# Two attention and MLP layers on one core: V of the first two token tiles from raw x, mended afterwards with column sums and norm rows

## The chip, the cores and the metric

The kernel runs on one core of one Trainium2 chip. The metric is the device time in microseconds (us) of one launch. Of the kernel before there are three runs with a median of 1616.25 us (1616.17 to 1616.3). A core has engines with instruction streams of their own: TensorE (PE) multiplies matrices into PSUM, VectorE (DVE), ScalarE (ACT) and GpSimd (POOL) work on vectors, SyncE (SP) issues most DMAs; ACT issues some too.

## The reference

x is 2048 tokens of D = 1024 in bf16. All is done twice, with the same weights:

```python
x = x + _A_ref(_layernorm(x), wqkv, wo)
x = x + _B_ref(_layernorm(x), W_gate, W_up, W_down)

# _A_ref: 32 heads of 32; each token looks at 8 keys: itself and 2, 4, ... 14 back
qkv = x @ wqkv                         # q, k, v
logits = einsum("bhsd,bhswd->bhsw", q, k[idx]) * Dh ** -0.5   # masked where idx < 0
o = einsum("bhsw,bhswd->bhsd", softmax(logits), v[idx])
return o @ wo
# _B_ref: F = 3584
h = relu(x @ W_gate) * (x @ W_up)
return h @ W_down

# _layernorm: (x - mean) / sqrt(var + 1e-5), no scale, no offset
```

## The kernel before

**Tiling.** The tokens lie in 4 blocks of 512, each of 4 tiles of 128 tokens; D lies in KC = 8 chunks of 128. x stays in SBUF, a token per partition. For a product the normalized block is turned, so that D lies on the partitions: xnT, 4 tiles x 8 chunks of 128x128. Blocks 1 to 3 are turned by DMA transposes on SP. Q, K and V come as [128 of D, 512 tokens] with a weight slab (1 MB, 512 columns or, for Q, K and block 0's V, half of the rows) as the stationary operand. The logits are 8 products of Q with a shifted K on DVE, added up over the head's dimensions: first in DVE (`prod_sum_steps`, tiles t, ac, s), then on PE by `head_mm`, eight products with a selection matrix into a two-bank PSUM tile L. `softmax_steps` does the softmax from L on DVE and ACT; `pv_steps` multiplies with V and sums on DVE; the result goes to DRAM (o_d) and comes back turned (oT) for the products with wo, whose results DVE adds to x.

**What sets the order.** All steps stand in a list `ev` with due times in us, in units of GRP = 1.73 (eight products of 512 columns); the list is sorted and emitted. Helpers keep each engine in that order: `dv` (L101) for DVE, `sp_dma` (L115) for SP, `pe_group` and `mm` (L124, L131) for PE, so that all products have line L132 in the profile, and most DVE operations L106. Weight slabs go through a ring of five buffers: a sixth is loaded when the first is free. PSUM has six one-bank tiles named "acc" (`psum`, taken in turn) and one two-bank tile "L" (`psum_l`), which scratch, turned tiles, bc and the logits share.

**The opening of block 0.** `load_x` brings tile 0's halves on SP and ACT, tile 1 on ACT. `load_slab` brings V's weights in eight pieces of 256 KB on SP, with tiles 2 and 3 of x between them, then Q's first half. `ln_first` (L318) holds the norm of block 0, `v_first` (L482) its V; the event `head` at 0.25 emits both:

- `open_up`: nine products of ones (`scratch`), which nothing reads; tile 0 is centred (mean only) in halves, turned by eight PE transposes (tp) and copied by ACT; tile 1 the same, with its turn between V products (tp_pair, tp_second).
- `chunk(kc, t)`: the eight 128-column V products of chunk kc, tile t. `halves`: both tiles at once, 256 columns.
- 1/sqrt(var) of tiles 0 and 1, split in three bf16 parts (`thirds`), is spread to all partitions by six products with the identity (`spread_rstd`, tile bc, copy rb). `scaled` multiplies V of tiles 0 and 1 with rb as it leaves PSUM; `widen` does the same to xnT for Q and K.
- tiles 2 and 3 are normalized in full (`apply`), turned on PE (tp_pair, 8 transposes each), and copied; tile 3's turn stands in the middle of tile 2's products, sixteen products ahead of where its data is used.

Behind it on PE: Q and K of block 0 (from t_qk0, 128 products), Q and K of block 1, V of blocks 1 and 2, with `head_mm(0)` in the middle of V of block 2 (due at t_v2 + 5.2 GRP), V of block 3, Q and K of block 2 in part, and wo of block 0.

Of the kernel before, what the change touches and what calls it, by code (L numbers as in the profile page):

```python
# [7 lines left out]
BF16 = mybir.dt.bfloat16  # L8
# [9 lines left out]
W = 8  # L18
# [18 lines left out]
def kernel(  # L37
# [123 lines left out]
    k_d = dram.tile([KC, P, S], BF16, name="k_d")  # L161
    s_d = [dram.tile([P, TPB, W, P], BF16, name=f"s_d{i}") for i in range(2)]
# [59 lines left out]
    def load_slab(key, src):  # L222
        shp = list(src.shape)
        t = wring.tile([P, 8 * SLAB], BF16, tag="slab", name="w_" + "_".join(str(k) for k in key))
        tv = t[:, 0:shp[1] * shp[2]].rearrange("p (a b) -> p a b", b=shp[2])
        if key[0] == "v0":
            for i, (k0, k1) in enumerate(((0, 1), (1, 2), (2, 3), (3, 4)) if key[1] == 0 else ((0, 1), (1, 2), (2, 3), (3, 4))):
                if (key[1], i) == (1, 2):
                    load_x(0, [2, 3])
                sp_dma(tv[:, k0:k1, :], src[:, k0:k1, :])  # L230
        else:
            sp_dma(tv, src)
        slab[key] = tv
# [84 lines left out]
    def ln_first():  # L318
        hold = {"xnT": xnT_pool.tile([P, TPB, KC, P], BF16, tag="xnT", name="xnT_first")}
        xna = big_tile([P, TPB, D], "xn_first", True)  # L320
        last = {}
# [20 lines left out]
        def aggr(t):  # L342
            mv = stat_pool.tile([P, 2], F32, tag="mv", name="mv", bufs=4)
            on("v", nc.vector.bn_aggr, mv[:], bst[t][:].rearrange("p a b -> p (a b)"))
            mean[t] = mv[:, 0:1]
            power(t, mv[:, 1:2], 1.0)

        pair = stat_pool.tile([P, 2], F32, tag="rpair", name="rpair", bufs=1)

        def power(t, var, sign):  # L350
            vpe = small("vpe1")
            rstd[t] = pair[:, t:t + 1] if t < 2 else small("rstd1")[:]
            on("g", nc.gpsimd.tensor_scalar, vpe[:], var, sign, EPS, op0=ALU.mult, op1=ALU.add)
            on("g", nc.gpsimd.tensor_tensor, rstd[t], vpe[:], neg_half[:, 0:1], op=ALU.pow)

        def centre():
            parts = [small("part0"), small("part1")]
            on("v", nc.vector.tensor_scalar, xna[:, 0, 0:SLAB], x_tiles[0][:, 0:SLAB], 1.0 / D, None, op0=ALU.mult,
               op1=ALU.add, accum_out=parts[0][:])
            on("a", nc.scalar.activation, xna[:, 0, SLAB:D], x_tiles[0][:, SLAB:D], ACT.Identity, scale=1.0 / D,  # L360
               accum_out=parts[1][:])
            for h in range(2):
                cols = slice(h * SLAB, (h + 1) * SLAB)
                on("v", nc.vector.tensor_scalar, xna[:, 0, cols], x_tiles[0][:, cols], parts[0][:], parts[1][:],
                   op0=ALU.subtract, op1=ALU.subtract)

        def centre_second():
            for h in range(2):
                cols = slice(h * SLAB, (h + 1) * SLAB)
                on("v", nc.vector.tensor_scalar, xna[:, 1, cols], x_tiles[1][:, cols], mean[1], None, op0=ALU.subtract)  # L370

        def square_of(src):
            sq = small("sq1")
            on("a", nc.scalar.activation, xna[:, 3, :], src, ACT.Square, scale=float(D) ** -0.5, accum_out=sq[:])
            return sq

        def act_mean(t):
            mn = small("mean1")
            on("a", nc.scalar.activation, xna[:, t, :], x_tiles[t][:], ACT.Identity, scale=1.0 / D, accum_out=mn[:])
            mean[t] = mn[:]  # L380

        def act_power(t, sq):
            nvar = small("nvar1")
            on("v", nc.vector.scalar_tensor_tensor, nvar[:], mean[t], mean[t], sq[:], op0=ALU.mult, op1=ALU.subtract)
            power(t, nvar[:], -1.0)

        def thirds():
            parts, rest = [], pair
            for i in range(3):
                part = pool["early"].tile([P, 2], BF16, tag=f"part{i}", name=f"part{i}", bufs=1)  # L390
                on("g", nc.gpsimd.tensor_copy, part[:], rest[:])
                parts.append(part)
                if i < 2:
                    left = stat_pool.tile([P, 2], F32, tag="left", name="left", bufs=2)
                    on("g", nc.gpsimd.tensor_tensor, left[:], rest[:], part[:], op=ALU.subtract)
                    rest = left
            return parts

        def spread_rstd():
            hold["rb"] = pool["early"].tile([P, 2, P], F32, tag="rb", name="rb", bufs=1)  # L400
            bc = psum_l.tile([P, W, P], F32, tag="L", name="bc")
            with pe_group():
                for t in range(2):
                    for i, part in enumerate(hold["thirds"]):
                        mm(bc[:, t, :], lhsT=_ap(part, t, [[0, P]]), rhs=ident[:], start=(i == 0), stop=(i == 2))
            on("v", nc.vector.tensor_copy, hold["rb"][:], bc[:, 0:2, :])

        def widen():
            for t in range(2):
                on("v", nc.vector.tensor_tensor, hold["xnT"][:, t, :, :], hold["xnT"][:, t, :, :],  # L410
                   _ap(hold["rb"], t * P, [[0, KC], [1, P]]), op=ALU.mult)

        def apply(t, half=None):
            cols = slice(0, D) if half is None else slice(half * SLAB, (half + 1) * SLAB)
            on("v", nc.vector.tensor_scalar, xna[:, t, cols], x_tiles[t][:, cols], mean[t], rstd[t],
               op0=ALU.subtract, op1=ALU.mult)
# [3 lines left out]
        def turn(t, halves=(0, 1)):  # L420
            if t in tps:
                pass
            elif t == 0:
                tps[t] = [psum.tile([P, KC // 2, P], BF16, tag="acc", name=f"tp{h}")[:] for h in range(2)]
            else:
                both = psum_l.tile([P, 2, KC, P], BF16, tag="L", name="tp_pair")
                tps[t] = [both[:, h, 0:KC // 2, :] for h in range(2)]
                if t == 1:
                    tps[t][1] = psum.tile([P, KC // 2, P], BF16, tag="acc", name="tp_second")[:]
            for c in (h * (KC // 2) + i for h in halves for i in range(KC // 2)):  # L430
                with pe_group():
                    tail_pe[0] = nc.tensor.transpose(tps[t][c // (KC // 2)][:, c % (KC // 2), :],  # L432
                                                     xna[:, t, c * P:(c + 1) * P], ident[:]).ins

        def copy(t, eng, h, i0=0, i1=KC // 2):
            f = nc.vector.tensor_copy if eng == "v" else nc.scalar.copy
            on(eng, f, hold["xnT"][:, t, h * (KC // 2) + i0:h * (KC // 2) + i1, :], tps[t][h][:, i0:i1, :])

        def open_up():
            warm = small("warm")  # L440
            on("a", nc.scalar.activation, warm[:], ones[:, 0:1], ACT.Identity)
            scratch(9)
            centre()
            turn(0)
            copy(0, "a", 0, 0, KC // 4)
            copy(0, "a", 0, KC // 4, KC // 2)
            copy(0, "a", 1)
            bn(1, 0)
            bn(1, 1)
            aggr(1)  # L450
            centre_second()
            power(0, square_of(xna[:, 0, :])[:], 1.0)
            hold["thirds"] = thirds()

        hold.update(on=on, bn=bn, aggr=aggr, apply=apply, turn=turn, copy=copy, widen=widen,
                    spread_rstd=spread_rstd, open_up=open_up, last=last, square_of=square_of, act_mean=act_mean,
                    act_power=act_power)
# [24 lines left out]
    def v_first(ln):  # L482
        st = att[0]
        pairs, opened = {}, set()

        def prod(kc, c, t0, t1):
            part = t0 // 2
            if (part, c // 2) not in pairs:
                pairs[part, c // 2] = psum.tile([P, 2, BLK // 2], F32, tag="acc", name="acc_v")
            acc = pairs[part, c // 2][:, c % 2, (t0 % 2) * P:(t0 % 2 + t1 - t0) * P]  # L490
            with pe_group():
                mm(acc, lhsT=slab["v0", kc // (KC // 2)][:, kc % (KC // 2), c * P:(c + 1) * P],
                   rhs=ln["xnT"][:, t0:t1, kc, :], start=(part, c // 2) not in opened, stop=(kc == KC - 1),
                   skip_group_check=True)
            opened.add((part, c // 2))

        def scaled(i):
            dv(nc.vector.tensor_tensor, st["vT"][:, 2 * i:2 * i + 2, 0:2 * P], pairs[0, i][:],
               _ap(ln["rb"], 0, [[0, 2], [1, 2 * P]]), op=ALU.mult)

        def later(t):
            ln["turn"](t)
            ln["copy"](t, "a", 0)
            ln["copy"](t, "a", 1)

        def halves(i, part, k0):
            for c in (2 * i, 2 * i + 1):
                for kc in range(k0, KC):
                    prod(kc, c, 2 * part, 2 * part + 2)

        def head():
            st["vT"] = big_tile([P, KC, BLK], "vT_0", True)
            ln["open_up"]()

            def chunk(kc, t):
                for c in range(KC):
                    prod(kc, c, t, t + 1)

            for kc in range(3):
                chunk(kc, 0)  # L520
            ln["turn"](1, (0,))
            ln["copy"](1, "v", 0)
            chunk(3, 0)
            ln["turn"](1, (1,))
            ln["copy"](1, "a", 1)
            for kc in range(4):
                chunk(kc, 1)
            chunk(4, 0)
            chunk(4, 1)
# [3 lines left out]
            ln["spread_rstd"]()  # L533
# [628 lines left out]
```

## Time and profile before

| | |
|---|---|
| median of three runs | 1616.25 us |
| the profiled execution's span | 1614.4 us, 1.85 less than the median |
| PE busy | 1607.8 us (100%) |
| DVE, ACT, POOL busy | 1141.5, 474.9, 178.1 us |
| first V product starts | 6.03 us |
| first Q product starts | 22.0 us |
| block 0's logits on PE (L) | 101.52 us |
| first group of block 0's wo products | 157.33 us |

The profile is of one execution. Its page gives busy times and the chain of work that ended last; the trace answers with the same for a window (the chain in order of time; a timeline of groups, with start, length, engine, line, operation, out<-in, count and, in brackets, the idle time before and its releaser; a table of windows with the busy time of PE, PE's weight loads, DVE, ACT, POOL, then the granted PE clock, the DMA share and GB/s).

### The profile page before, as it was taken

The page shows a single profiled execution, that of the slowest core. Times are in us where ns is not written, and L with a number is a line of the kernel's source. Part 1 is how long each engine was busy: PE and PEld are TensorE (multiplying, and loading weights), DVE is VectorE, ACT ScalarE, POOL GpSimd, SP SyncE. Part 2 cuts the span into 40 slices and gives each one's busy share as a digit, 9 for nine tenths or more (in the row PEclk, how much of TensorE's full clock was granted, in tenths as well). Part 3 has the DMA queues.
Part 4 walks back from the last instruction along what each step waited for, and adds up shares of the span by engine and source line. Part 5 has one row for each costly group of instructions (what it writes and reads, how often), then busy time and mean ns, then how long its engine had stood idle before and what let it go on. Part 6 is the DMA issues. An engine that isn't in the chain of part 4 may idle for free.

```text
span 1614.4 us, 19048 instructions
## 1 busy us (share of the span) xinstructions
PE 1607.8 (100%) x7657; PEld 790.4 (49%) x7707; DVE 1141.5 (71%) x966; ACT 474.9 (29%) x968; POOL 178.1 (11%) x173
## 2 busy tenths in 40 slices
PE   9999999999999999999999999999999999999999
PEld 7646544444444445444454444544445444444445
DVE  6999979997989698929389393993939939311211
ACT  5753312131115313603136031361313311131110
POOL 2400000010003002300053000530005100000000
PEclk9999999999999999999999999999999999999999
DMA  9767867596668666784747857488574874655452
GB/s 305 186 195 243 215 180 237 184 229 199 201 199 222 197 188 201 201 244 146 227 157 204 235 157 232 151 200 254 165 226 157 205 240 157 210 157 181 157 167 68
DMA packets 359561, 317.94 MB, mean 197 GB/s; under 512 B 105136, under 2 KB 333616, under 8 KB 358960
## 3 DMA queue, kind: packets, MB, share of 16 engines
q1 hardware_dynamic: 358896, 316.13, 66.8%
q8 instruction: 60, 0.98, 0.3%
q10 hardware_dynamic: 576, 0.59, 0.1%
q14 instruction: 29, 0.24, 0.1%
HBM read 266.29 MB, written 34.66 MB: 186 GB/s over the span
## 4 chain that ended last, share of the span: by engine, by line
PE 99%; issue 0%; DVE 0%; DVEq 0%
PE acc_u L132 24%; PE acc_g L132 24%; PE dacc L132 18%; PE acc_v L132 7%; PE acc_k L132 7%; PE acc_q L132 7%; PE acc_wo L132 7%; PE dacc_pair L132 5%; PE scratch L132 0%; DVE x L915 0%; PE tp_pair L432 0%; PE tp L432 0%; PE L L132 0%; PE bc L132 0%; PE tp_second L432 0%
## 5 line engine op out<-in xcount | busy, mean ns | idle before, releaser
L132 PE MATMUL acc_u<-xnT_b,w_u 128*128 128x512 bf16 x1792 | 423.3, 379 | 0.0
L132 PE MATMUL acc_g<-xnT_b,w_g 128*128 128x512 bf16 x1792 | 423.3, 379 | 0.0
L858 ACT ACTIVATE r<-acc_g 128x512 bf16<-128x512 f32 x224 | 133.5, 596 | 724.8 <-PE acc_g L132 687.7
L106 DVE TENSOR_TENSOR hT<-acc_u,r 128x512 bf16<-128x512 f32 x224 | 150.8, 686 | 240.9 <-PE acc_u L132 238.1
L132 PE MATMUL dacc<-w_d,hT 128*128 128x512 bf16 (+2 forms) x1427 | 303.5, 369 | 1.5
L132 PEld LDWEIGHTS <-hT 128*128 128x128 bf16 x1876 | 181.3, 98 | 206.0
L132 PEld LDWEIGHTS <-w_g 128*128 128x128 bf16 x1792 | 175.4, 98 | 211.3
L132 PEld LDWEIGHTS <-w_u 128*128 128x128 bf16 x1792 | 175.3, 98 | 211.5
L106 DVE TENSOR_TENSOR pv<-a,vhm 128x4096 bf16<-128x4096 bf16 x64 | 143.5, 2283 | 0.0
L915 DVE TENSOR_TENSOR x<-dacc,x 128x512 bf16<-128x512 f32 (+2 forms) x40 | 24.9, 654 | 154.2 <-PE dacc L132 154.2
L671 DVE TENSOR_TENSOR t<-q,k 128x2048 f32<-128x2048 bf16 x56 | 128.0, 2292 | 6.7 <-ACT k L606 4.6
L106 DVE TENSOR_TENSOR t<-q,k 128x2048 f32<-128x2048 bf16 x56 | 127.4, 2285 | 3.1 <-ACT k L606 1.6
L106 DVE TENSOR_TENSOR pv<-pv 128x1024 bf16<-128x1024 bf16 (+1 forms) x128 | 113.7, 949 | 0.0
L132 PE MATMUL acc_wo<-w_o,oT 128*128 128x512 bf16 x498 | 111.1, 379 | 0.7
L687 DVE TENSOR_TENSOR ac<-ac,t 128x2048 f32<-128x2048 f32 x48 | 109.7, 2285 | 0.3
L106 DVE TENSOR_TENSOR ac<-ac,t 128x2048 f32<-128x2048 f32 x48 | 109.6, 2283 | 0.0
L612 POOL COPY kh<-k 128x14 bf16<-128x14 bf16 x40 | 51.7, 1296 | 502.3 <-ACT k L606 502.3
L265 POOL TENSOR_TENSOR st_b<-st_b,neg_half 128x1 f32<-128x1 f32 x29 | 43.6, 1511 | 528.5 <-ACT st_b L264 528.5
L132 PE MATMUL dacc_pair<-w_d,hT 128*128 128x512 bf16 (+1 forms) x413 | 92.5, 372 | 0.4
L132 PEld LDWEIGHTS <-oT 128*128 128x128 bf16 x512 | 50.1, 98 | 60.4
L260 ACT ACTIVATE xn_b<-x 128x1024 bf16<-128x1024 bf16 x29 | 30.3, 1045 | 131.3 <-DVE x L106 69.2
L477 ACT CAST vT<-acc_v 128x512 bf16<-128x512 f32 x56 | 32.5, 587 | 57.6 <-PE acc_v L132 56.7
(151 smaller groups left out, 1236.0 us busy)
## 6 DMA issues: line engine op xcount, KB each, us to landing
w_g<-in_B_W_gate_dram SPq DMA_DIRECT2D x56, 1024.0 KB, 7.2
w_u<-in_B_W_up_dram SPq DMA_DIRECT2D x56, 1024.0 KB, 5.5
w_d<-in_B_W_down_dram SPq DMA_DIRECT2D x48, 1024.0 KB, 6.1
w_o<-in_A_wo_dram SPq DMA_DIRECT2D x16, 1024.0 KB, 8.1
vhm<-v_d SPq DMA_DIRECT2D x32, 284.0 KB, 6.8
v_d<-vT SPq DMA_DIRECT2D x8, 1024.0 KB, 9.5
oT<-o_d SPq DMA_DIRECT2D x32, 256.0 KB, 3.8
w_d<-in_B_W_down_dram SPq DMA_DIRECT2D x16, 512.0 KB, 3.7
```

The costliest lines, as they stand in the source:

```text
L106: tail_dve[0] = f(*args, **kwargs).ins
L132: tail_pe[0] = nc.tensor.matmul(*args, **kwargs).ins
L260: nc.scalar.activation(xn, xt[:], ACT.Square, accum_out=sq)
L265: nc.gpsimd.tensor_tensor(rstd, vpe, neg_half[:, 0:1], op=ALU.pow)
L477: tail_act[0] = nc.scalar.copy(st["vT"][:, c, :], acc[:]).ins
L612: nc.gpsimd.tensor_copy(khalo[n][:, c, :], k[:, BLK:BLK + HALO])
L671: nc.vector.tensor_tensor(t[:], i0, i1, op=ALU.mult)
L687: nc.vector.tensor_tensor(o, i0, i1, op=ALU.add)
L858: tail_act[0] = nc.scalar.activation(rs[j][:], acc[:], ACT.Relu).ins
L915: run = dv if n < NB - 2 else (lambda f, *args, **kwargs: f(*args, **kwargs))
```

## The change

V of tiles 0 and 1 is computed from raw x. With W the weights, m the mean and r = 1/sqrt(var + eps) of a token, V = r (x W - m colsum(W)).

- Raw x is turned by ordinary products with the identity (x as the stationary operand), to f32 PSUM, and copied to `xr` in bf16. Tile 1's right operand has one column of ones more (129 columns), so that its products bring the column sums of W.
- Five scratch products instead of nine. Tile 0 and 1 are multiplied one after the other for every chunk: 128 products of 128 or 129 columns, no 256-column ones. `keep` copies their sums from PSUM to SBUF (`raw`, f32, and `cols`) by ACT.
- `put_rows`: -m and r of both tiles (`st4`, 128x4) are split in three bf16 parts and turned by three products into a PSUM tile of 4x128, copied by DVE, and stored to DRAM (`st_d`) by a DMA of ACT. `get_rows` reads the four rows back to all partitions (512 runs of 512 bytes), also on ACT.
- `mend`: DVE adds -m colsum (eight operations of 128x256) and multiplies with r (four of 128x512).
- Tiles 0 and 1 for Q and K are normalized by `apply` and turned by two DMA transposes on SP (`turn_dma`). `centre`, `spread_rstd`, `scaled`, `widen` go.
- Turns of tiles 2 and 3 move: tile 2's between the products of tiles 0 and 1, tile 3's behind all first-half products of tile 2; what comes behind it is tile 3's first half.
- x of tiles 2 and 3 is loaded before the first and the last of V's second four pieces, no longer both together before the third; block 1's first two tiles of x get due times 0.35 and 0.45. Block 1's statistics, apply and turns are due 3.9 us later. `head_mm(0)` and `softmax_steps(0)` are due 2 GRP later: sixteen products of V of block 2 come ahead of the logits that came behind them.

The core of the diff:

```diff
+    st_d = dram.tile([4, P], F32, name="st_d")
...
+        xr = work.tile([P, KC, 2 * P + 2], BF16, tag="t", name="xr_first")
+        nc.gpsimd.memset(xr[:, :, 2 * P:2 * P + 2], 1.0)
...
+        def put_rows():
+            acc = psum.tile([4, P], F32, tag="acc", name="acc_rows")
+            for i, part in enumerate(hold["thirds"]):
+                with pe_group():
+                    mm(acc[:], lhsT=part[:], rhs=ident[:], start=(i == 0), stop=(i == 2))
+            short = pool["early"].tile([4, P], F32, tag="short", name="short", bufs=1)
+            on("v", nc.vector.tensor_copy, short[:], acc[:])
+            on("a", nc.scalar.dma_start, st_d[:], short[:])
+
+        def get_rows():
+            hold["rows"] = pool["early"].tile([P, 4, P], F32, tag="rows", name="rows", bufs=1)
+            on("a", nc.scalar.dma_start, hold["rows"][:],
+               bass.AP(tensor=st_d.tensor, offset=st_d.offset, ap=[[0, P], [P, 4], [1, P]]))
+
+        def turn_dma(t):
+            sp_dma(hold["xnT"][:, t, :, :], xna[:, t, :], True)
...
-            scratch(9)
-            centre()
+            scratch(5)
             turn(0)
-            copy(0, "a", 0, 0, KC // 4)
-            copy(0, "a", 0, KC // 4, KC // 2)
+            copy(0, "v", 0)
             copy(0, "a", 1)
+            bn(0, 0)
+            bn(0, 1)
...
+        def mend(i):
+            for c in (2 * i, 2 * i + 1):
+                dv(nc.vector.scalar_tensor_tensor, st["raw"][:, c, :], ln["rows"][:, 0:2, :].rearrange("p a t -> p (a t)"),
+                   st["cols"][:, c:c + 1], st["raw"][:, c, :], op0=ALU.mult, op1=ALU.add)
+            dv(nc.vector.tensor_tensor, st["vT"][:, 2 * i:2 * i + 2, 0:2 * P], st["raw"][:, 2 * i:2 * i + 2, :],
+               _ap(ln["rows"], 2 * P, [[0, 2], [1, 2 * P]]), op=ALU.mult)
...
+            chunk(0, 0)
             ln["turn"](1, (0,))
             ln["copy"](1, "v", 0)
-            chunk(3, 0)
+            chunk(1, 0)
             ln["turn"](1, (1,))
             ln["copy"](1, "a", 1)
+            chunk(0, 1)
+            chunk(1, 1)
+            for kc in range(2, KC - 2):
+                for t in range(2):
+                    chunk(kc, t)
+            ln["aggr"](0)
+            ln["bn"](1, 0)
+            ln["bn"](1, 1)
+            ln["aggr"](1)
             ln["bn"](2, 0)
             ln["bn"](2, 1)
             ln["aggr"](2)
+            ln["thirds"]()
+            for t in range(2):
+                ln["apply"](t)
+                ln["turn_dma"](t)
             ln["apply"](2)
+            ln["bn"](3, 0)
+            for t, i in ((0, 0), (1, 0), (0, 1), (None, 0), (1, 1), (1, 2)):
+                if t is None:
+                    ln["turn"](2)
+                    ln["copy"](2, "v", 0)
+                    ln["copy"](2, "v", 1)
+                    continue
+                for c in range(PER[t] * i, min(PER[t] * (i + 1), KC)):
+                    for kc in range(KC - 2, KC):
+                        raw_prod(kc, c, t)
+                keep(t, i)
+            ln["bn"](3, 1)
+            ln["aggr"](3)
             for t in (2, 3):
                 for c in range(KC):
                     for kc in range(KC // 2):
                         prod(kc, c, t, t + 1)
+                    if (t, c) == (2, 1):
+                        ln["put_rows"]()
+                        ln["apply"](3)
+                if t == 2:
+                    ln["turn"](3)
+                    ln["copy"](3, "a", 0)
+                    ln["copy"](3, "a", 1)
+                    ln["get_rows"]()
             for i in range(KC // 2):
+                mend(i)
...
-    ev.append((t_v2 + 5.2 * GRP, lambda: head_mm(0)))
-    spread(softmax_steps(0), t_v2 + 5.3 * GRP, 0.01)
+    ev.append((t_v2 + 7.2 * GRP, lambda: head_mm(0)))
+    spread(softmax_steps(0), t_v2 + 7.3 * GRP, 0.01)
```

## The prediction

> **What bounds the kernel now.** I read the page's busy times and chain first, then the waits of TensorE (PE), then the chain of the first 60 us, where the change works, then the timelines of VectorE (DVE) and PE, and the table of windows, between the two places where block 0's attention meets PE.
>
> ```profile
> span 1614.4 us, 19048 instructions
> PE 1607.8 (100%) x7657; PEld 790.4 (49%) x7707; DVE 1141.5 (71%) x966; ACT 474.9 (29%) x968; POOL 178.1 (11%) x173
> PE 99%; issue 0%; DVE 0%; DVEq 0%
> ```
>
> PE is the span: 6.6 us of 1614.4 are not PE work. A saved PE microsecond is worth one at most, and any hole torn into PE costs its full length. What lies around the span is 1616.25 − 1614.4 = 1.85 us; I add differences of the span straight to the median.
>
> ```profile
> 1.13 4.02 PE scratch L132 x9
> 5.15 0.85 PE tp L432 x8
> 6.03 1.62 PE acc_v L132 x24
> 7.65 0.22 PE tp_pair L432 x4
> 11.23 0.34 PE bc L132 x6
> 15.99 6.17 PE acc_v L132 x80
> 22.16 5.18 PE acc_q L132 x24
> ```
>
> The chain of the opening (start, length): nine scratch products, 0.427 us each, fill the time until x is centred; a 128-column product takes 107 ns until about 6.2 us and 56 ns from there (0.22 for four, 0.34 for six); 256 columns take 109 ns. V's first product starts at 6.03, Q's first at 22.0. All holes up to there make 0.24 us, so this opening is dense.
>
> **What leaves PE.** Four scratch products: 4 x 0.427 = 1.71. Six bc products: 0.34. Three row products come: 0.17. Sixteen transposes become sixteen identity products of the same width: nothing by count. Sixteen products of 256 columns become 32 of 128: 32 x 56 − 16 x 109 ns = +0.05. Net −1.83 us, which is the most that the change could bring.
>
> **The opening, laid out again.** Durations are DVE copies of 512 f32 PSUM columns 0.68, ACT copies 0.59, a PSUM drain 0.22 before a reader starts, bn_stats 0.68, apply 0.55 (all from the timeline of before).
> - Scratch ends at 1.13 + 5 x 0.427 = 3.26. x of tile 0 landed at 3.40 (issued 0.81), so the eight identity products run from 3.47 to 4.32: a hole of 0.2.
> - The first V product needs DVE's copy of the first four (3.90 + 0.22 + 0.68 = 4.83) and w_v's first piece (landed 4.86, same place in the queue): 4.9, a hole of 0.6. This is 1.1 us ahead of 6.03.
> - Eight V products and four identity products of tile 1 at 107 ns: 6.19. Eight at 56: 6.64. Tile 1's other four write the same PSUM tile that DVE is still to read; DVE has two bn_stats ahead (4.85 to 6.15), copies 6.44 to 7.13, so they start at 7.17: a hole of 0.5.
> - 4 + 112 + 8 products (the rest of tiles 0 and 1, tile 2's turn) x 56 ns: 14.1. The w_v pieces land 0.67 apart (the last at 11.69, wanted about 11.9), so they just hold.
> - DVE's copy of tile 2: 0.13. 32 products of tile 2 and the rows' three: 16.2.
> - Turn of tile 3 stands right behind and needs apply(3). On DVE this lies behind tile 2's copies, half of bn(3), aggr and POOL's power (0.56): 16.8, a hole of 0.6. Eight turns: 17.3. Then the ACT copy (0.22 + 0.59), with nothing on PE between: before puts 16 products there, the change none. Hole 0.85, to 18.15.
> - 32 x 56 + 32 x 109 ns = 5.28: Q starts at 23.4, where before has 22.0. The opening **loses 1.4 us**: 2.9 us of holes and a few more half-rate products against the 1.83 taken out.
>
> **Behind the opening: SP's queue.** The rows of block 1's transposes in before (count, shortest, median and longest hold of the queue in ns; below, us from issue to landing):
>
> ```profile
> L121 SPq DMA_TRANSPOSE xnT_a<-xn_a x4: 1250/2869/4042, 24.9 to 33.4; - x4
> DMA to landing us min/median/max: 2.8/5.7/7.0
> ```
>
> Two such transposes now stand on SP for tiles 0 and 1: the queue is held for 1.25 to 4.0 us each, after apply(0) at about 10.7. Behind them wait w_qk_q's second half, block 1's x, w_qk_k and w_qk_k's second half. With 2.9 each the second q half issues at about 17 and lands near 20.4 (bounds 19.5 and 27); Q's second half wants it at 24.3. xnT of tiles 0 and 1 lands at 16.6 and 17.7 (at 7.0 us to landing, 21 to 22) and is wanted at 23.4. I take no cost, and 0 to 2.9 for the range. DVE's two widen multiplications leave (2.35).
>
> **DVE: rows and mend.** Three row products, their copy (15.6), a write to DRAM and a read back by ACT, which waits between them with nothing urgent behind it. No row shows this: the shortest transfers of the opening took 2.6 us (x), zpad's 28 KB 6.9. I take 3.5 each, near x of tile 1 with w_v in flight (3.8): rows land at 22.8 (20.9 to 29.5). Mend: eight at 0.38 to 0.41 (128x256) and four at 0.66: 5.3, over at 28.1. Statistics and apply of block 1's four tiles stand behind it on DVE: 4 x 2.2 = 8.8, so block 0's scores start at 36.9, not 30.69. Its fifteen operations per half take 33.9 us dense (67.29 to 101.18); before's first half took 36.6, so 2.7 are won back: s ends at 36.9 + 67.8 = 104.7.
>
> **The head's logits, moved two groups later.** From the timelines of DVE and PE, start and length:
>
> ```profile
> 98.89 2.29 DVE L106 TENSOR_TENSOR s<-ac,t 128x2048 bf16<-128x2048 f32 x1
> 102.19 0.27 DVE L106 TENSOR_TENSOR L<-L,maskc 32x112 f32<-32x112 f32 x1 [1.00 <-PE L L132]
> 101.52 0.61 PE L132 MATMUL L<-s,sel 128*32 128x512 bf16 x8
> ```
>
> In before s ends at 101.18 and PE's L products start at 101.52: PE is there when s is. In the change head_mm goes from 5.2 to 7.2 groups: 16 products of 512 columns are passed, 16 x 0.2158 = 3.45 us. L then starts at 101.52 + 1.4 + 3.45 = 106.4, and s at 104.7 has 1.7 us of air: the delay that the mend puts on DVE is what the move makes room for. PE loses nothing at this place. But DVE does its softmax, P·V and block 1's scores behind L (the window from L to the first x add; DVE's waits in it; the two instructions that meet at its end):
>
> ```profile
> 101.52:167.58 66.06, 66.01 (x312) 37.87 (x313) 63.99 (x50) 20.28 (x34) 0.00 (x0) 1.00 0.72 215
> DVE ssum L106 <- ACT d L732: 1.1, 1, 1.1
> 166.89 0.68 DVE L106 TENSOR_TENSOR x<-acc_wo,x 128x512 bf16<-128x512 f32 x1
> 167.69 0.59 PE L132 MATMUL acc_wo<-w_o,oT 128*128 128x512 bf16 x2
> ```
>
> From L to the end of the first x add DVE is busy 63.99 of 66.06 us (fourth column); its only waits are L itself and 1.1 on ACT's exponential. The x add ends at 167.57, and it empties the first of six PSUM banks, which the seventh wo group (167.69) needs: 0.11 us of slack. So what DVE falls behind PE between these two places, PE waits here: 3.45 − 0.11 = **3.35 us**. About 2 us of it may already show a little earlier, since w_o's first half (landed 159.02, wanted 160.78) stands in SP's queue behind o stores and loads that come from DVE; it is the same lag and isn't added. After 172 us the order is that of before, and nothing gives it back.
>
> **Sum:** 1.4 + 3.35 = +4.75; 1616.25 + 4.75 = **1621.0** (span 1619.1). About 0.2% of it, 3.2 us, is what a measurement of this kernel can tell from no change.
>
> **Rivals.**
> 1. *Not slower.* The seventh wo group doesn't wait for the first x add, because DVE makes up the lag between L and there; then only the opening is left: 1616.25 + 1.4 = 1617.7, within 0.2%. It decides from 3.35 us of air on DVE between L and 167.57. For: the softmax's reductions wait 1.1 on ACT. Against: 2.07 us idle in 66, none that a late L shortens. 15%, and 3% on top that holes close too and the 1.83 come out (1614.4 to 1616).
> 2. *The clock.* Before runs at half rate until it has been busy 5.1 us from 1.13 with no hole; the change has holes to 7.17. If the 5.1 count from the last hole, full rate comes at 12.3, and 48 products cost 51 ns more: +2.45, 1623.4. Against: the holes are 0.2 to 0.6 us, and the granted clock is 1.00 in every stretch of before, later holes included. 10%. The Trainium skill ("TensorE: Matmul & The Clock Gate", Part 1) has full rate granted at the edge of a free-running activity window of about 3.4 us; an estimate by that page: if the window that ends at 6.26 counts as too idle, the next ends at 9.67, 27 products lie between, 27 x 51 ns = 1.4 us, 1622.4. The trace of before, which has one edge, can't separate the two.
> 3. *The rows are late.* With 5.7 us per transfer (the transposes' median to landing) s comes 4.4 later than at 3.5, 2.7 beyond L's place, and L waits on PE: 1623.7. It decides from 1.7 us. For: two transfers and an ACT wait in series amid slab loads. 12%.
> 4. *SP is held.* Both transposes take 4.0 and land late, q's second half at 27: up to 2.9 of PE hole, 1623.9. 10%.
>
> **How the numbers follow.** Forecast 50%, rivals 18 (1), 10, 12, 10. The forecast's own range is 1619.6 to 1622.3 (opening 0 to +2.7). Rivals 2 to 4 reach 1624 and partly add up; rival 1 lies at 1617.7. Range 1617.4 to 1625.0. Slower by over 0.2%: forecast and rivals 2 to 4, 82%, less 2 for an opening that comes out even; within 0.2%: 17%; faster by over 0.2% needs more than the 1.83 us that leave PE: 3% at most, kept at 2.
>
> **What would show it.** In the changed kernel's chain: five scratch, V's first product near 4.9, Q's first at 23.4; PE waits for DVE at tile 1's second four and at tile 3's turn, for ACT behind it. L on PE at about 106.4, with s done before. Then one wait of PE near 160 to 169, for DVE's x or w_o, about 3.35 in all. Wrong it is if PE has no wait over 1 us there, if Q starts by 22.2, or if L waits for s.

## The result, and the profile after

The changed kernel takes 1626.92 us (median of five runs, 1623.69 to 1629.01) against 1616.25: ratio 1.0062, 95% interval 1.0049 to 1.0074. It is slower by 10.7 us, as forecast in sign, but 2.2 times the forecast 4.75, and above the range. The five runs lie 5.3 us apart; those of before 0.3. TensorE's granted clock (the share of full speed) was 1.000 in the two shortest, 1623.69 and 1624.2, and 0.999 or 0.998 in the three longer ones, so the longer runs are those with the lower clock.

The profiled execution is the slowest of the five (1629.01, span 1627.3, 12.9 more than before). The page's busy times and its chain:

```profile
span 1627.3 us, 19131 instructions
PE 1614.6 (99%) x7716; PEld 791.8 (49%) x7716; DVE 1145.1 (70%) x976; ACT 471.6 (29%) x964; POOL 182.0 (11%) x176
PE 89%; DVE 8%; DMA 2%; SPq 0%; issue 0%; ACT 0%; POOL 0%; DVEq 0%; ACTq 0%
```

The chain now runs through DVE for 8% of the span, 130 us, and through DMA for 2%. The waits of PE that bear on this (total, times, longest); before had only one, 1.1 for the scratch products' ones:

```profile
PE L L132 <- DVE s L106: 3.3, 1, 3.3
PE acc_wo L132 <- DVE x L106: 2.0, 1, 2.0
PE acc_v L132 <- ACT xnT_first L332: 0.7, 1, 0.7
PE raw L132 <- DMA w_v<-in_A_wqkv_dram: 0.7, 1, 0.7
PE acc_wo L132 <- DMA w_o<-in_A_wo_dram: 0.5, 1, 0.5
```

Where that chain begins is seen in the chain of the first 60 us, which has no PE left in it from 15.3 us on (start, length):

```profile
16.87 0.15 DVE short L106
17.04 4.79 DMA st_d<-short
21.85 6.49 DMA rows<-st_d
28.39 0.05 issue
28.44 0.90 DVE raw_first L106 x2
...
34.61 1.21 DVE bst L106 x2
...
43.38 2.28 DVE ac L106
```

The rows take 4.79 us out and 6.49 back; DVE stands idle for 10 us, mends until 34.5, does block 1's statistics behind that, and block 0's scores start at 43.38 instead of 30.69. The timelines of DVE and PE at the two places where attention meets PE:

```profile
109.34 2.29 DVE L106 TENSOR_TENSOR s<-ac,t 128x2048 bf16<-128x2048 f32 x1
107.97 0.40 PE L132 MATMUL L<-s,sel 128*32 128x512 bf16 x4
111.68 0.62 PE L132 MATMUL L<-s,sel 128*32 128x512 bf16 x4 [3.31 <-DVE s L106]
178.62 5.30 PE L132 MATMUL acc_wo<-w_o,oT 128*128 128x512 bf16 x16 [2.04 <-DVE x L106]
```

s ends at 111.63, 10.4 later than before, and 3.3 after PE has come to L's second half. The first x add ends at 178.57, 11.0 later. The rest is the clock: the last line's sixteen products take 5.30 us instead of 3.6. From 180.05 to 183.33 they start 0.427 us apart, not 0.216, and so do those from 112.2 to 115.1, behind the first wait. The table of windows shows it in the granted clock, the third column from the end:

```profile
105.00:108.00 3.00, 3.00 (x19) 1.21 (x17) 3.00 (x2) 0.79 (x2) 0.00 (x0) 1.00 0.41 121
111.60:113.00 1.40, 1.32 (x6) 0.39 (x6) 0.65 (x3) 0.00 (x0) 0.00 (x0) 0.50 1.06 264
180.00:184.00 4.00, 4.00 (x13) 1.62 (x12) 3.20 (x8) 3.18 (x9) 1.10 (x2) 0.60 0.43 117
```

The first K product behind wo starts at 183.76 instead of 171.14: 12.6 later, which is 11.0 of DVE's lag and 1.6 of slow products. The span's 12.9 adds 0.3 to that; nothing is given back.

### The profile page after: what moved, and what is told of

Read it like the earlier page. It is cut to its first block, busy times and chain, and to the rows that moved or that the text cites. A ratio compares the mean times of both kernels' runs of the same rounds, so it can differ in the third digit from the quotient of the medians.

```text
span 1627.3 us, 19131 instructions
## 1 busy us (share of the span) xinstructions
PE 1614.6 (99%) x7716; PEld 791.8 (49%) x7716; DVE 1145.1 (70%) x976; ACT 471.6 (29%) x964; POOL 182.0 (11%) x176
## 4 chain that ended last, share of the span: by engine, by line
PE 89%; DVE 8%; DMA 2%; SPq 0%; issue 0%; ACT 0%; POOL 0%; DVEq 0%; ACTq 0%
PE acc_g L132 24%; PE acc_u L132 24%; PE dacc L132 18%; PE acc_wo L132 6%; PE dacc_pair L132 5%; PE acc_k L132 4%; PE acc_v L132 4%; PE acc_q L132 3%; DVE ac L106 2%; DVE t L106 2%; DVE pv L106 2%; PE raw L132 0%; DMA rows<-st_d 0%; DMA w_v<-in_A_wqkv_dram 0%; DVE bst L106 0%; DMA st_d<-short 0%
```

## The experiments

Theory A: the rows' trip through DRAM holds up DVE, and DVE's lag at s and at the first x add sets the time. Theory B: the opening and the moved logits set it, as the prediction's sum has it.

**Rows without DRAM.** The edit:

```diff
-            acc = psum.tile([4, P], F32, tag="acc", name="acc_rows")
...
-                    mm(acc[:], lhsT=part[:], rhs=ident[:], start=(i == 0), stop=(i == 2))
...
-            on("a", nc.scalar.dma_start, st_d[:], short[:])
...
-                    ln["get_rows"]()
...
+            acc = psum.tile([P, 4, P], F32, tag="acc", name="acc_rows")
+            with pe_group():
+                for j in range(4):
+                    for i, part in enumerate(hold["thirds"]):
+                        mm(acc[:, j, :], lhsT=_ap(part, j, [[0, P]]), rhs=ident[:], start=(i == 0), stop=(i == 2))
+            hold["rows"] = pool["early"].tile([P, 4, P], F32, tag="rows", name="rows", bufs=1)
+            on("v", nc.vector.tensor_copy, hold["rows"][:], acc[:])
```

> The changed kernel, but the four norm rows don't go through DRAM: twelve products with the identity (instead of three) spread them to all partitions, and DVE copies that PSUM tile. Theory A (the late rows hold up DVE, and DVE's lag sets the time): the rows are there near 18 us instead of 28.4, block 0's scores start near 33 instead of 43.4, s ends near 102 and L has no wait for it; left are the opening (about 3.0) and the moved logits (about 3.35): 1622.6 us, and the runs lie closer together than 1623.7 to 1629.0. Theory B (the rows cost nothing of their own, the opening and the order behind it do): unchanged, 1626 to 1627.

Measured 1622.39 us (1622.16 to 1623.56; ratio to before 1.0039, 1.0026 to 1.0051). s ends at 103.70 and PE starts L at 107.50 with no wait; what waits are left stand at wo:

```profile
PE acc_wo L132 <- DMA w_o<-in_A_wo_dram: 1.7, 1, 1.7
PE acc_wo L132 <- DVE x L106: 1.4, 1, 1.4
```

On medians the trip costs 4.5 us of the 10.7. The runs lie 1.4 apart, not 5.3. The two shortest runs of the changed kernel lie only 1.3 to 1.8 above this median, so the price varies from run to run; of these runs only the slowest was profiled.

**Logits early,** in the changed kernel:

```diff
-    ev.append((t_v2 + 7.2 * GRP, lambda: head_mm(0)))
-    spread(softmax_steps(0), t_v2 + 7.3 * GRP, 0.01)
+    ev.append((t_v2 + 5.2 * GRP, lambda: head_mm(0)))
+    spread(softmax_steps(0), t_v2 + 5.3 * GRP, 0.01)
```

> The changed kernel, but the logits of block 0 are due at 5.2 groups as before the change. Theory A: s ends where it did, near 108 to 111.6, PE only waits longer for it (about 6.5 instead of 3.3 us) and less at the first x add, DVE's path is the same: within 2 us of the changed kernel, 1625 to 1628. Theory B (the move itself costs 3.35): 1623.5.

Measured 1627.43 us (1625.88 to 1628.34): no better. PE comes to L at 103.90 and stands there longer, and there is no wait left at wo:

```profile
PE L L132 <- DVE s L106: 6.9, 1, 6.9
```

While s is late, L's place on PE neither costs nor saves: B's sum does not hold for the changed kernel.

**Before, with the logits alone moved:** the same four lines the other way round, in the kernel before.

> The kernel before with the one edit that the logits of block 0 and their softmax are due two groups later. By the prediction's step (DVE has 0.11 us of air between L and the first x add) PE waits 3.35 us at wo: 1619.6 us, or some 1.7 more if the granted clock falls behind that wait as it did in the changed kernel. By rival 1 of the prediction: 1616.3, no change.

Measured 1619.84 us (ten runs, 1619.65 to 1622.35; ratio 1.0027, 1.0017 to 1.0036), 3.6 more than before. The timeline of PE shows the wait where the prediction put it:

```profile
105.13 0.61 PE L132 MATMUL L<-s,sel 128*32 128x512 bf16 x8
161.60 7.08 PE L132 MATMUL acc_wo<-w_o,oT 128*128 128x512 bf16 x32 [0.50 <-DMA w_o<-in_A_wo_dram]
171.25 3.61 PE L132 MATMUL acc_wo<-w_o,oT 128*128 128x512 bf16 x16 [2.56 <-DVE x L106]
```

L is 3.6 later than in before, the waits at wo make 3.1, and the first K product behind wo is 3.55 later. In this execution the sixteen products behind the wait run at full rate. Six of the ten runs have a granted clock of 1.000 and take 1619.65 to 1619.92; the four with 0.999 or 0.998 take 1621.28 to 1622.35.

**Rows by PE and early logits together.**

> The changed kernel with both: rows spread by PE, logits due at 5.2 groups. Theory A: s ends near 102, L stands near 104.5 on PE, and DVE lags no more than PE does; left is the opening: 1616.25 + 3.0 = 1619.3 us. Theory B: 1623.5, as with the early logits alone. If s is later than L's place, each us of that is added.

Measured 1618.55 us (eleven runs, 1617.74 to 1619.5; ratio 1.0014, 1.0005 to 1.0023). L starts at 103.79, s has ended at 103.46, PE has no wait behind the opening:

```profile
PE scratch L132 <- DVE ones L311: 1.1, 1, 1.1
PE acc_v L132 <- ACT xnT_first L332: 0.7, 1, 0.7
PE raw L132 <- DMA w_v<-in_A_wqkv_dram: 0.6, 1, 0.6
```

Q starts 2.27 us later than in before (24.27 to 22.00) and the last product ends 2.27 later: with these two edits the opening is all that is left. Taken in this order, the medians give 2.3 for the opening, 3.84 for the moved logits (1622.39 − 1618.55) and 4.53 for the trip (1626.92 − 1622.39). That these make 10.7 is so by construction and shows nothing; in the other order the logits give nothing (1627.43) and the trip 8.9 (1627.43 − 1618.55). What speaks for the first two is that the logits cost 3.6 in the kernel before too, and that Q's delay is the whole delay here. They are what B counts; the trip it left out.

**Why the trip is long: fewer, longer runs.** The changed kernel, with the rows read back as 128 runs of 2 KB:

```diff
...
-               bass.AP(tensor=st_d.tensor, offset=st_d.offset, ap=[[0, P], [P, 4], [1, P]]))
+               bass.AP(tensor=st_d.tensor, offset=st_d.offset, ap=[[0, P], [1, 4 * P]]))
```

> The changed kernel, but the four rows are read back as 128 runs of 2 KB (a partition's four rows are one stretch of DRAM) instead of 512 runs of 512 bytes. Theory R1 (the small transfers wait behind the slab loads that were issued before them): the read still takes 6 to 6.5 us and lands near 28, no change: 1624 to 1629. Theory R2 (the many short runs are what is slow): the read takes about 3.5 us, s ends 3 us earlier, PE doesn't wait for L: 1623 to 1624.

Measured 1627.34 us (1624.68 to 1627.43); the read takes 6.7 us, as before. The short runs are not the cause.

**SP's slabs ahead of the transposes,** in the changed kernel:

```diff
-    ev.append((0.15, head))
+    ev.append((0.5, head))
```

> The changed kernel with the opening's event at 0.5 instead of 0.15: on SP Q's second half, K's first half and two tiles of x are issued ahead of the two transposes, not behind them; nothing else moves. Theory R1: these 2.5 MB land by about 22 instead of 26.7, so the write of the rows (issued near 17) still lands near 21 but their read no longer has 1 MB ahead of it: rows near 25, s near 108, 1622.5 to 1625. Theory R2: unchanged, 1624 to 1629. Risk to both: the transposes land later than xnT is wanted (24 us), a hole before Q.

Measured 1628.35 us (1626.2 to 1628.95). The write was over sooner, at 19.87, but the read still took 6.8 us (26.68), beside K's half (landed 21.65), x (22.30) and the transposes. Those now land at 24.67 and 26.93, and the risk named came true:

```profile
PE acc_q L132 <- DMA xnT_first<-xn_first: 3.4, 1, 3.4
PE acc_wo L132 <- DVE x L106: 3.2, 1, 3.2
```

R1's number (rows near 25) was missed by 1.7; the run does not tell whether slabs or transposes kept the read. Nor did the time come out as R1 had it (1622.5 to 1625).

**The same trip where little else runs.** A second write and read of that shape behind the first x adds of the last block, at 1597.5 us; nothing uses what it brings:

```diff
+    trip_d = dram.tile([4, 2 * P], BF16, name="trip_d")
...
+                if n == NN - 1 and half == 0:
+                    nc.scalar.dma_start(trip_d[:], x_tiles[b * TPB][0:4, 0:2 * P])
+                    nc.scalar.dma_start(x_tiles[0][:].rearrange("p (a t) -> p a t", a=4),
+                                        bass.AP(tensor=trip_d.tensor, offset=trip_d.offset,
+                                                ap=[[0, P], [2 * P, 4], [1, 2 * P]]))
```

> The changed kernel with a second trip through DRAM of the same shape (four runs of 512 bytes out, 512 runs of 512 bytes back to all partitions, both on ACT) near 1590 us, where hardly any other transfer is under way; nothing uses what it brings. Theory R1 (the trip of the opening waits behind the slab loads): the second write takes about 2 us and the second read 2.5 to 3.5, against 4.8 and 6.5 in the opening. Theory R3 (128 partitions that read the same 2 KB of DRAM take that long whatever else runs): the second read takes 6 to 7 us too. The time is that of the changed kernel, 1624 to 1629.

1628.38 us in its one run. The trace's answer for that tile:

```profile
L936 ACTq DMA_DIRECT2D trip_d<-x x1: 273/273/273, 1597.5 to 1597.5; - x1
L937 ACTq DMA_DIRECT2D x<-trip_d x1: 353/353/353, 1599.2 to 1599.2; - x1
...
DMA to landing us min/median/max: 3.4/3.4/3.4
```

1.7 us from the write's issue to the read's, then 3.4: 5.1, against 11.3 in the opening. The shape is not slow, the place is: from 17 to 28.4 us of the changed kernel the sixteen DMA engines are full (mean busy share 1.02), from 1597.5 to 1602.6 us here it is 0.62. Whether the bytes issued ahead or those moved beside it make the trip long, no run tells apart. The Trainium skill ("DMA: Bandwidth & Descriptors", Issuing engines are not separate DMA queues) says that transfers of all issuing engines run on the same sixteen DMA engines; that these two, alone on ACT's queue, took twice as long beside SP's slabs agrees with it.

**The mend behind block 1's statistics,** in the changed kernel, and the same with early logits:

```diff
-            for i in range(KC // 2):
-                mend(i)
...
-        return head
+        return head, lambda: [mend(i) for i in range(KC // 2)]
...
-    head = v_first(ln_a[0])
+    head, mends = v_first(ln_a[0])
...
+    ev.append((t_v0 + 17.7, mends))
```

> The changed kernel, rows through DRAM, but DVE's mend stands behind the statistics and three of the four applies of block 1 instead of ahead of them. The trip is as long as it was (rows near 28). Theory A': what the late rows cost is the 10 us that DVE stands idle with block 1's statistics queued behind the mend: now these fill the wait, scores start near 35 instead of 43.4, s ends near 103.5, ahead of L's place: 1622.4 us as with rows by PE. Theory A'' (whatever needs the late rows, V itself, is late for its own users): 1626 to 1627.

> The same with block 0's logits due at 5.2 groups as before the change. By A': left are the opening and what s comes late for L's place: 1618.6 to 1619.5. By A'': 1627.

Measured 1624.6 us (1624.31 to 1626.12) and 1626.34 us (1625.12 to 1626.4): 2.3 and 1.1 less than the same kernels with the mend ahead, where 4.5 and about 8 were expected. Neither gain is clear of the spread of these kernels' runs (5.3 and 2.5 us). The timeline of DVE of the first shows why there isn't more:

```profile
21.89 1.28 DVE L106 BATCH_NORM_STATS2 bst<-x 128x6 f32<-128x512 bf16 x2 [3.70 <-DMA x<-in_A_x_dram]
26.49 1.29 DVE L106 BATCH_NORM_STATS2 bst<-x 128x6 f32<-128x512 bf16 x2 [2.89 <-DMA x<-in_A_x_dram]
30.65 1.29 DVE L106 BATCH_NORM_STATS2 bst<-x 128x6 f32<-128x512 bf16 x2 [1.99 <-DMA x<-in_A_x_dram]
41.35 2.29 DVE L106 TENSOR_TENSOR ac<-q,k 128x2048 f32<-128x2048 bf16 x1
```

Block 1's x lands at 21.9, 26.5, 30.6 and 31.3 (before: 18.8, 19.5, 25.5, 26.2), because its loads stand on SP behind the two transposes (10.5 to 15.7) and the slabs behind these. So DVE waits 8.6 us for x, and scores start at 41.35, not near 35. In the changed kernel the wait for the rows hides this second delay; with rows by PE and early logits the mend stands in that time. Theory A' was right that block 1's statistics can fill the wait (scores start 2.0 earlier), and wrong in taking block 1's x as there. By the second run's time A'' (1627) is nearer.

**The opening: a filled hole, and another order.** In the kernel with both edits: (1) the first part of this diff; (2) the second part, with `head` at 0.5; (3) both parts, with `head` at 0.15:

```diff
+        return sc
...
-            scratch(5)
+            sc = scratch(5)
             turn(0)
+            for _ in range(6):
+                with pe_group():
+                    mm(sc[:, 0, :], lhsT=ones[:], rhs=ones[:], start=True, stop=True)
...
                     if (t, c) == (2, 1):
-                        ln["put_rows"]()
                         ln["apply"](3)
                 if t == 2:
                     ln["turn"](3)
+                    ln["put_rows"]()
```

> The changed kernel with rows spread by PE and early logits (1618.55), and six more 128-column products of ones, which nothing reads, in the hole between the first eight identity products and the first V product. Theory K1 (the full clock waits for a stretch without such holes): full rate starts near 6.3 instead of 8.5, about 20 products save 51 ns: 1617.5. Theory K2 (the clock's time has nothing to do with that hole): full rate near 8.5 to 9.2, 1618.5, or a little more if the products delay the first V product.

> The changed kernel with rows spread by PE, early logits, the opening's event at 0.5 as in the run on SP's order, and the twelve row products moved from tile 2's V products to behind tile 3's turn, where PE waited 0.7 for ACT's copy and 0.4 for DVE's apply. If these holes are what is left of the opening's loss: Q starts near 23.6 instead of 24.3, 1617.9. If the transposes now land after 23.6, or s ends after L's place, each us of that is added.

> The kernel of the filled hole (1618.04), with the row products moved behind tile 3's turn, SP's order as in the change. The holes of 0.7 and 0.4 close, the transposes land near 17 as there: Q starts near 22.8 instead of 23.5, 1617.3 us. s may end 0.5 late, since the rows come 2 us later: then 1617.8. Faster than before is not expected.

Measured 1618.04 (1617.63 to 1618.91), 1620.05 (1619.88 to 1620.7) and 1617.86 (1617.62 to 1618.09; ratio to before 1.001, 1.0001 to 1.0019). In (2) the hole of 0.7 behind tile 3's turn is gone, one of 0.7 ahead of it is left, and Q waits 2.1 us for the transposes, as in the run on SP's order. In (3) Q starts at 23.70. No version beats the kernel before, and (1) does not settle the clock: full rate was there at 5.84, but at 5.12 in (2), which has the hole unfilled.

## Why the prediction was wrong

**What failed: the rows' price.** "I take 3.5 each" stood for 7.0; measured 4.79 and 6.49, and the write issued at 17.04, not 15.7. The mend took 6.1 instead of 5.3 (0.48 us for each 128x256 operation, forecast 0.38 to 0.41). Scores therefore started at 43.4, not 36.9, s ended at 111.6, not 104.7, and the "1.7 us of air" ahead of L became a wait of 3.3: "L waits for s" was one of the prediction's own signs of being wrong. The nearest row was not x of tile 1 (3.8), which left at 1.25 when only tile 0's halves had been issued, but zpad's 28 KB (6.9), issued at 23.03 in the same crowd of slabs. The rows' bounds held (28.3, within 20.9 to 29.5), the choice between them was wrong.

**What followed from it: the sum.** Opening and moved logits were added along PE. They are what is left only while s comes before L. With s late, DVE's chain from the rows to the first x add is the path and covers both (logits early: no change). The total then comes out 4.5 above what the two alone make on medians. That the sign was right is no proof of the sum: the path that set the time was not the one it followed.

**Rival 3** was what happened: 5.7 per transfer, 11.4 in all, was its price (measured 11.3), 2.7 of wait at L (3.3), 1623.7. Two terms kept it below 1626.9: the opening was longer, and the products behind a wait ran at half rate (1.6 us behind the first x add in the profiled run), which no step of the prediction has. The range stopped at 1625.0 although rivals 2 and 3 "partly add up": they did.

**The opening** was right in kind, 1.4 forecast and 3.0 in the profile (2.3 with both edits). Four of its five holes were found; the 0.5 forecast for DVE's copy at tile 1's second four is not there, because the V product ahead of them waited 0.65 for w_v's second piece. V's first product started at 5.29, forecast 4.9, since x landed at 3.86; that piece came at 7.34, where before's came at 5.80. And rival 2 came true in part: full rate began at 9.15 instead of 6.2, 20 products lie between, 20 x 51 ns = 1.0 us. Its count of 5.1 us from the last hole, which ended at 7.39, would give 12.5 and did not come. With the hole filled, and full rate at 5.84, Q started at 23.49, near the forecast's 23.4; that kernel has 15 small products more (six in the hole, nine for the rows), so the nearness is partly luck.

**The moved logits** were right: 3.35 forecast from 0.11 us of air at the first x add, 3.6 measured alone in the kernel before (3.4 to 3.7 with the clock whole), with the wait at the seventh wo group. Rival 1 falls with that.

**SP's queue** cost PE nothing, as forecast: Q waits for no transfer, and the transposes landed at 17.1 and 18.0, forecast 16.6 and 17.7. But block 1's x behind them was counted for PE only and not for DVE, whose statistics need it; that delay of 3 to 7 us is hidden by the larger one.

## What to carry to other kernels

A small transfer can take twice as long where the DMA engines are full (11.3 us against 5.1 here): price it by a row from the same moment and load, not by its size. Where two engines meet twice, follow the lag of each of them between the meetings, and add up along one path only; the other's delays are covered. Taking away the longest wait shows the next one, so look ahead of time at what stands behind it (here the x loads behind the transposes).

## What the runs showed of the hardware

Two waits of PE were followed by a stretch at half rate: behind 3.3 us of waiting from the resumption to 115.06; behind 2.04 us of waiting full rate for 1.5 us and then half rate from 180.05 to 183.33. The granted clock changes in steps. In the changed kernel it is 0.50 from 111.50 to 114.91 and from 179.77 to 183.18, one step of 3.413 us each; the two starts lie 20 such steps apart, and full rate's start at 9.10 another 30 ahead. In all fourteen profiles the changes of one execution lie whole steps of that length apart. Windows cut at the steps show what goes ahead of half rate (PE's busy time is the first number behind the window's length); the first four lines are of the changed kernel, the last two of the first run with the late mend:

```profile
108.09:111.50 3.41, 0.28 (x4) 0.00 (x0) 3.38 (x2) 0.57 (x1) 0.00 (x0) 1.00 0.56 192
111.50:114.91 3.41, 3.23 (x11) 1.14 (x11) 2.62 (x4) 0.00 (x0) 0.00 (x0) 0.50 0.92 232
176.35:179.77 3.42, 1.38 (x8) 0.55 (x6) 3.42 (x5) 0.00 (x0) 0.00 (x0) 1.00 0.85 91
179.77:183.18 3.41, 3.41 (x10) 1.23 (x9) 2.61 (x7) 3.12 (x8) 0.57 (x2) 0.50 0.26 61
173.68:177.10 3.42, 1.52 (x8) 0.69 (x8) 3.42 (x5) 0.34 (x1) 0.00 (x0) 1.00 0.39 41
177.10:180.51 3.41, 3.41 (x17) 1.93 (x16) 2.61 (x7) 2.78 (x8) 0.94 (x2) 1.00 0.52 158
```

Up to the end of PE's work, each of the eight full-rate steps of these profiles in which PE was busy for 1.38 us or less was followed by half rate, and none with 1.52 us or more. So it matters where a wait falls: 2.04 us within one step cost 1.6 us more, while no half rate followed 2.56 us in before with the logits moved (1.2 and 1.36 in two steps), nor even the 3.43 us ahead of Q in the run with SP's slabs first (1.68 and 1.75). The Trainium skill ("TensorE: Matmul & The Clock Gate", Part 1) has the clock decided in free-running windows of about 3.4 us, half rate after an idle one: the length agrees, but 2.04 us of idling were enough here.

The steps begin elsewhere in each execution (full rate first comes at 4.83 to 9.84), so runs of one kernel can differ; that this makes the spread of the changed kernel's five runs is likely, and not shown. In the opening no single share of busy time decides: steps with PE busy for 2.89 us or less left the clock at half, those with 2.97 or more ended it, but the changed kernel's own from 5.69 to 9.10, with 2.76, ended it too. The column of the granted clock reads 1.00 from 0 to 6 us of before, though products there take twice their later time: in the opening, the spacing of products has to be read, not this column.
